# A start-order planner of a fused attention and two-layer kernel: double cost for transfers to 64 partitions, and a hold on transfers while the modelled queue is long

## The chip, the cores and the metric

One core of one Trainium2 chip. The metric is the device time of one execution in microseconds (us). The engines are called as in the profile: PE (TensorE, matmuls), PEld (its weight loads), DVE (VectorE), ACT (ScalarE), POOL (GpSimd) and SP (SyncE, which issues nearly all transfers).

## The reference

```
q, k, v: 4 x 8 x 576 x 64     s: 4 x 8 x 576
cum    = cumsum(max(s, 0))
scores = q k^T / 8 + min(cum_j - cum_i, 0), causal, then a softmax over j
x      = (attn v), heads side by side: 2304 tokens x 512
h = x w_in  (512 x 2048);  g = softplus(h);                 y   = g w_out
h = y w_in2 (512 x 2048);  g = P(h)/Q(h) (cubic/quadratic); out = g w_out2
```

All inputs are large enough in scale that the softmax is sharp. The kernel keeps matmul operands as a high part and a low part, so most products are three matmuls.

## The kernel before, in words

**Work.** 32 (batch, head) pairs of attention produce x. The first layer (`ph` 0) takes the tokens in six tiles, two of 256 and four of 448; the second (`ph` 1) takes six tiles of 384. Per tile and per block of 128 hidden columns (`ff`, 16 of them) `stage_a` (L990) makes h with 12 matmuls (L1006 to L1008), `stage1` and `stage3` the nonlinearity and its split (L1104 to L1108, L1144, L1146), `stage_b` (L1028) the second product (L1042 to L1044; L1049 to L1051 in the second layer). Attention runs alongside the first layer: the first 256 rows of batches 0 and 1 come first, since the two tiles of 256 tokens need nothing else; the other heads are spread between the blocks. A head is `scores` (L607 to L610), `softmax_rows` (DVE L587 to L602, ACT L600, POOL L603), transposes (L673 to L694) and the product with v (L732, L757).

**What arrives by transfer.** `load_pair` (L499) brings q and k of two early heads to 64 partitions (256 KB), `load_cum` (L504) two rows of running sums below them (`raw2<-cumc`, 8 KB), `load_v2` the v of eight heads (768 KB). `load_raw` (L519, transfer at L539) brings q and k of the later heads to all 128 partitions; `prep` adds rows of sums (`st<-cum_d`, L563). `load_w` (L847, transfer at L856) brings 512 KB of weights as 64-bit floats to 128 partitions; `conv_t` (L862, DVE L870 and L872, ACT L871) makes them 32-bit, and `conv_hl` splits them (ACT L881, POOL L882); low parts go out to memory at L891 and come back at L901.

**What sets the order.** The program text gives instructions and dependences. `plan` (L318) then simulates the first 600 us with costs of its own: `Step` gives each instruction a duration, `forward` (L207) starts at each step the ready instruction that can start first, by rank among equals, and `latest` (L292) makes new ranks from the latest start that each could have had. Six rounds are run and the shortest is kept. L1335 chains the instructions of every engine in that order; each engine, SP among them, runs its list in order on the chip. The planner's transfers share one line, `dma`: each starts when the line is free and takes bytes / `DMA_RATE`, and lands `DMA_LATENCY` later (L272). In `earliest` (L225) a transfer may not start before the eighth last one has landed (`LANES`). All these numbers act on the order alone.

Of the kernel before, what the change touches and what calls it, by code (L numbers as in the profile page):

```python
# [59 lines left out]
SHARED = {("two", "wide"): 0.7, ("two", "thin"): 0.25, ("one", "wide"): 0.7, ("one", "thin"): 0.3,  # L60
          ("wide", "two"): 0.2, ("wide", "one"): 0.05, ("thin", "two"): 0.6, ("thin", "one"): 0.3}
HOLD, ROUNDS = 0.0, 6
DMA_RATE, DMA_LATENCY, LANES = 320e3, 1.9, 8


class Access:


    def __init__(self, x):
        t = x.bass_ap.tensor  # L70
        dims = [tuple(d) for d in x.bass_ap.ap]
        self.tile, self.dims, off = t.name, dims, x.bass_ap.offset
        self.elements = 1
        for _, m in dims[1:]:
            self.elements *= m
        self.pool = self.psum = None
        if getattr(t, "tag_meta", None) is None or str(t.space).endswith("DRAM"):
            self.box = (0, 1, off, off + sum(s * (n - 1) for s, n in dims) + 1)
            self.ordered = "_d" in t.name
            return  # L80
        self.ordered = True
        self.pool = (str(t.tag), t.tag_meta.bufs)
        self.psum = str(t.tag).split("_")[0] in PSUM_TAGS
        row = 1
        for n in list(t.shape)[1:]:
            row *= n
        p0, f0 = divmod(off, row)
        self.box = (p0, p0 + dims[0][1], f0, f0 + sum(s * (n - 1) for s, n in dims[1:]) + 1)
        if self.psum:
            self.box = (0, 128, 0, 512)  # L90
# [10 lines left out]
class Step:  # L101


    def __init__(self, i, tied):
        self.i, self.tied = i, tied
        self.engine = str(i.engine).split(".")[-1]
        acc = [[Access(x) for x in xs if getattr(getattr(x, "bass_ap", None), "tensor", None) is not None]
               for xs in (i.outs, i.ins)]
        self.outs, self.ins = acc
        self.dma, self.port = 0, None  # L110
        n = self.outs[0].elements if self.outs else 1
        psum = any(x.psum for x in self.outs + self.ins)
        wide = len(self.ins) > 1 and self.ins[1].dims[1][1] > 1
        if "DMA" in i.opcode:
            self.dma = 4 * n * self.outs[0].dims[0][1]
            self.busy = self.done = ISSUE.get(self.engine, 0.5)
        elif self.engine == "PE":
            turn = self.ins[0].tile.startswith("ident")
            full = not turn and "32r" not in str(i.ins[0].bass_ap.dtype)
            self.busy = 0.00085 * n if turn else 0.024 + 0.00162 * n if full else 0.012 + 0.000428 * n  # L120
            self.done = self.busy + 0.165
        elif self.engine == "Activation":
            more = max(0, len(self.outs) + len(self.ins) - 2)
            near = any(x.psum for x in self.ins)
            self.busy = (0.12 + 0.00079 * n + 0.07 * more) if near else (0.165 + 0.0008 * n + 0.095 * more)
            self.done = self.busy + 0.08
        elif self.engine == "DVE" and n == 1:
            self.busy, self.done = 0.115, 0.155
        elif self.engine == "DVE":
            one = len(self.ins) < 2 and not psum and i.opcode != "TensorCopy"  # L130
            self.busy = 0.06 + 0.00064 * n if one else 0.107 + 0.00105 * n
            self.done = self.busy + 0.06
            self.port = None if psum else "one" if one else "two"
        elif self.engine == "Pool":
            self.busy = 0.22 + 0.00205 * n if wide else 0.28 + 0.0007 * n
            self.done = self.busy + 0.03
            self.port = "wide" if wide else "thin"
        else:
            self.busy = self.done = 0.1
# [39 lines left out]
class Planner:  # L179
# [27 lines left out]
    def forward(self, rank):  # L207
        steps, tiles, pool, queue = self.steps, self.tiles, self.pool, self.queue
        n = len(steps)
# [13 lines left out]
        dma, landed = 0.0, []  # L223

        def earliest(k):  # L225
            t, need = ready[k], {}
            if steps[k].dma and len(landed) >= LANES:
                t = max(t, landed[-LANES])
            for x in tiles[k]:
                if x not in held:  # L230
                    tag = pool[x][0]
                    need[tag] = need.get(tag, 0) + 1
                    ahead = queue[tag][head[tag]:head[tag] + need[tag]]
                    if any(y not in held and y not in tiles[k] for y in ahead):
                        return None
                    free = sorted(slots[tag], key=lambda q: q[0])
                    if len(free) < need[tag]:
                        return None
                    t = max(t, free[need[tag] - 1][0], last[tag])
            return t  # L240

        for _ in range(n):
            best = None
            for e in self.engines:
                can = [(max(t, clock[e]), rank[k], k) for k in wait[e] for t in (earliest(k),) if t is not None]
                if can:
                    t0 = min(can)[0]
                    pick = min((c for c in can if c[0] <= t0 + HOLD), key=lambda c: (c[1], c[0], c[2]))
                    if best is None or pick[0] < best[0]:
                        best = pick  # L250
            t, _, k = best
# [19 lines left out]
            if s.dma:  # L271
                dma = max(dma, clock[s.engine]) + s.dma / DMA_RATE  # L272
# [1123 lines left out]
```

## Time and profile before

| | |
|---|---|
| Median of 3 runs | 1045.41 us (1045.2 to 1045.7) |
| The profiled execution | 1044.85 us |
| Its span, first to last instruction | 1043.1 us |
| Instructions | 17736 |
| PE busy | 1018.0 us, 98% of the span |
| DVE, ACT, POOL busy | 784.5, 803.5, 459.4 us |
| Transfers | 138.70 MB, mean 133 GB/s |

The profiled execution is 0.56 us under the median and 1.75 us over its own span. Busy shares are averages over stages; the table of stretches tells the stages apart. A busy PE is not PE at its peak, since matmuls are pipelined and their ends are modelled. In rows of instructions the columns are start, duration, engine, line, operation, output and inputs, and in brackets the idle time of the engine before it with what ended it.

### The profile page before, as it was taken

Reading aid. Unit: us, or ns where it says so; the run is one execution under the profiler, and the core shown is the slowest. Engines: PE = TensorE matmul, PEld = TensorE weight load, DVE = VectorE, ACT = ScalarE, POOL = GpSimd, SP = SyncE. Lnnn points to the kernel's source line nnn. Section 1 sums busy time; section 2 is a strip of 40 time slices with the busy share of each in tenths; the row PEclk is TensorE's granted clock in tenths of the full one; section 3 lists DMA queues with packets and bytes.
Section 4 is the critical chain, followed back from the end, with each engine's and each line's share of the span. In section 5 each row is a group of like instructions: output and inputs, shape, how many; then the busy total and the mean of one; then the engine's idle time right before and its main releaser. Section 6 shows DMA issues by size and latency. Waiting matters only on the chain.

```text
span 1043.1 us, 17736 instructions
## 1 busy us (share of the span) xinstructions
PE 1018.0 (98%) x5764; PEld 923.3 (89%) x5764; DVE 784.5 (75%) x1858; ACT 803.5 (77%) x1693; POOL 459.4 (44%) x509
## 2 busy tenths in 40 slices
PE   6999999999999999999999999999999999999998
PEld 5889989988998888999999999989999999999996
DVE  5888877788887888885776787687676776767765
ACT  5898878887887778786566567778787887887875
POOL 2756765421221122222435775445454454444542
PEclk9999999999999999999999999999999999999999
DMA  8877566565564644435779865010010110100100
GB/s 237 298 244 240 171 211 209 176 202 155 167 180 129 207 151 139 129 107 175 246 231 324 301 181 194 1 31 31 1 62 1 31 31 1 44 18 1 31 1 31
DMA packets 67950, 138.70 MB, mean 133 GB/s; under 512 B 8336, under 2 KB 21456, under 8 KB 67856
## 3 DMA queue, kind: packets, MB, share of 16 engines
q1 hardware_dynamic: 65312, 133.39, 40.6%
q10 hardware_dynamic: 2544, 4.16, 1.5%
q8 instruction: 46, 0.75, 0.3%
q14 instruction: 48, 0.39, 0.1%
HBM read 110.82 MB, written 22.61 MB: 128 GB/s over the span
## 4 chain that ended last, share of the span: by engine, by line
PE 71%; DVE 12%; ACT 6%; DMA 4%; POOL 3%; issue 3%; SPq 0%; POOLq 0%; DVEq 0%; ACTq 0%
PE h L1007 6%; PE h L1006 6%; PE h L1008 6%; PE at L732 5%; PE acc L1049 5%; PE acc L1051 5%; PE acc L1050 5%; PE acc L1043 4%; PE acc L1042 4%; PE acc L1044 4%; PE at L1006 3%; PE at L1007 3%; PE at L1008 3%; PE at L609 3%; PE at L610 2%
## 5 line engine op out<-in xcount | busy, mean ns | idle before, releaser
L1006 PE MATMUL h<-xs,w1h 128*128 128x448 f32 (+1 forms) x352 | 120.1, 342 | 1.3 <-DVE e L1108 1.3
L1043 PE MATMUL acc<-gl,w1h 128*128 128x448 f32 (+1 forms) x352 | 119.4, 341 | 1.2 <-POOL gl L1146 1.2
L1007 PE MATMUL h<-xs,w1h 128*128 128x448 f32 (+1 forms) x352 | 119.5, 340 | 0.0
L1008 PE MATMUL h<-xs,w1l 128*128 128x448 f32 (+1 forms) x352 | 119.4, 340 | 0.0
L1042 PE MATMUL acc<-gh,w1h 128*128 128x448 f32 (+1 forms) x352 | 119.3, 341 | 0.0
L1044 PE MATMUL acc<-gh,w1l 128*128 128x448 f32 (+1 forms) x352 | 118.2, 338 | 0.1
L603 POOL TENSOR_SCALAR PA<-PA,stat 128x384 f32<-128x384 f32 (+3 forms) x112 | 71.9, 648 | 101.5 <-DVE stat L602 33.6
L1049 PE MATMUL acc<-w2h,gh 128*128 128x512 f32 x288 | 113.9, 395 | 0.1
L1051 PE MATMUL acc<-w2h,gl 128*128 128x512 f32 x288 | 113.5, 394 | 0.0
L1050 PE MATMUL acc<-w2l,gh 128*128 128x512 f32 x288 | 113.5, 394 | 0.0
L1146 POOL TENSOR_TENSOR gl<-PA,gh 128x384 fp32r<-128x384 f32 x95 | 96.7, 1018 | 6.2 <-ACT gh L1144 5.0
L1117 POOL TENSOR_TENSOR tc<-tc,e 128x384 f32<-128x384 f32 x47 | 50.8, 1082 | 98.5 <-ACT tc L1115 98.5
L603 POOL TENSOR_SCALAR P<-P,stat 128x576 f32<-128x576 f32 x32 | 26.4, 824 | 136.2 <-DVE stat L602 36.0
L600 ACT ACTIVATE PA<-PA,stat 128x384 f32<-128x384 f32 (+3 forms) x112 | 64.0, 572 | 11.5 <-DVE stat L587 9.3
L1006 PEld LDWEIGHTS h<-xs,w1h 128*128 128x128 f32 x352 | 66.3, 189 | 5.4 <-DVE e L1108 1.7
L1043 PEld LDWEIGHTS acc<-gl,w1h 128*128 128x128 f32 x352 | 66.1, 188 | 4.7 <-POOL gl L1146 1.4
L1007 PEld LDWEIGHTS h<-xs,w1h 128*128 128x128 f32 x352 | 66.2, 188 | 3.3
L1008 PEld LDWEIGHTS h<-xs,w1l 128*128 128x128 f32 x352 | 66.2, 188 | 3.3
L1044 PEld LDWEIGHTS acc<-gh,w1l 128*128 128x128 f32 x352 | 66.1, 189 | 3.4 <-POOL w1l L882 0.3
L1042 PEld LDWEIGHTS acc<-gh,w1h 128*128 128x128 f32 x352 | 66.1, 189 | 3.2
L1051 PEld LDWEIGHTS acc<-w2h,gl 128*128 128x128 f32 x288 | 54.1, 188 | 13.1 <-DVE gl L1146 0.3
L1130 DVE SCALAR_TENSOR_TENSOR tc<-tc,e 128x384 f32<-128x384 f32 x48 | 27.5, 574 | 50.4 <-ACT e L1129 48.6
(235 smaller groups left out, 3209.0 us busy)
## 6 DMA issues: line engine op xcount, KB each, us to landing
w1l<-l_d SPq DMA_DIRECT2D x138, 256.0 KB
raw<-in_w_dram SPq DMA_DIRECT2D x48, 512.0 KB
raw<-in_qk_dram SPq DMA_DIRECT2D x24, 384.0 KB
l_d<-w1l SPq DMA_DIRECT2D x32, 256.0 KB
raw64x<-in_w_dram SPq DMA_DIRECT2D x16, 512.0 KB
raw<-in_qk_dram SPq DMA_DIRECT2D x8, 576.0 KB
w_d<-PA SPq DMA_DIRECT2D x16, 256.0 KB
R<-in_vv_dram SPq DMA_DIRECT2D x12, 320.0 KB
```

Of the source, the lines that this page charges most:

```text
L600: nc.scalar.activation(pt[:, 0:n], pt[:, 0:n], AF.Exp, bias=mn, scale=-1.0, accum_out=stat[:, i, 1:2])
L603: nc.gpsimd.tensor_scalar(pt[:, 0:n], pt[:, 0:n], stat[:, i, 2:3], 1.0, op0=ALU.mult, op1=ALU.mult)
L1006: nc.tensor.matmul(h, wh[:, cs], xh, start=(k == 0), stop=False)
L1007: nc.tensor.matmul(h, wh[:, cs], xl, start=False, stop=False)
L1008: nc.tensor.matmul(h, wl[:, cs], xh, start=False, stop=(k == KD - 1))
L1042: nc.tensor.matmul(o, wh[:, cs], gh, start=first and not both, stop=False)
L1043: nc.tensor.matmul(o, wh[:, cs], gl, start=False, stop=False)
L1044: nc.tensor.matmul(o, wl[:, cs], gh, start=False, stop=last and (not both or m % 2 == 1))
L1049: nc.tensor.matmul(acc[m], gh[:, cs], wh, start=first, stop=False)
L1050: nc.tensor.matmul(acc[m], gh[:, cs], wl, start=False, stop=False)
L1051: nc.tensor.matmul(acc[m], gl[:, cs], wh, start=False, stop=last)
L1146: eng.tensor_tensor(gl, g, f(gh), op=ALU.subtract)
```

## The change

Three edits in the planner, none in the kernel's own instructions. The rate of its transfer line goes from 320e3 to 400e3 bytes per us. A transfer whose output has 64 to 127 rows counts double bytes: the pair loads and the few transfers that write half a tile. And a transfer may not start until the line's end is at most 1.5 us ahead (`BACKLOG`), so that in the simulation a transfer that becomes ready meanwhile can go first.

```diff
-DMA_RATE, DMA_LATENCY, LANES = 320e3, 1.9, 8
+DMA_RATE, DMA_LATENCY, LANES, BACKLOG = 400e3, 1.9, 8, 1.5
...
         if "DMA" in i.opcode:
-            self.dma = 4 * n * self.outs[0].dims[0][1]
+            rows = self.outs[0].dims[0][1]
+            self.dma = 4 * n * rows * (2 if rows in range(64, 128) else 1)
...
         def earliest(k):
             t, need = ready[k], {}
-            if steps[k].dma and len(landed) >= LANES:
-                t = max(t, landed[-LANES])
+            if steps[k].dma:
+                t = max(t, dma - BACKLOG)
+                if len(landed) >= LANES:
+                    t = max(t, landed[-LANES])
```

No instruction is added or removed; the five engines' lists are permuted. Of some 5600 instructions of PE the moves end at about the 3000th, and few are over 35 places; SP's list is the same in most of its second half. Three places follow. Lines of the changed file below the edits are 3 higher than before.

SP near the start of the program, before, and then with the change. `raw64_...` are weights, `raw2_...` early pairs (64 rows) and their rows of sums (2 rows, from `cumc`), `prm` the six coefficients of the second layer:

```order
L856 DMA raw64_1874<-in_w1_dram 128x1024
L856 DMA raw64_2030<-in_w1_dram 128x1024
L1326 DMA prm_125<-in_ab_dram 128x6
L505 DMA raw2_133<-cumc_149 2x1024
L505 DMA raw2_135<-cumc_149 2x1024
L505 DMA raw2_137<-cumc_149 2x1024
L501 DMA raw2_331<-in_qk0_dram 64x1024
L505 DMA raw2_331<-cumc_149 2x1024
L856 DMA raw64_165<-in_w1_dram 128x1024
L856 DMA raw64_167<-in_w1_dram 128x1024
L501 DMA raw2_429<-in_qk0_dram 64x1024
```

```order
L859 DMA raw64_1874<-in_w1_dram 128x1024
L508 DMA raw2_133<-cumc_149 2x1024
L508 DMA raw2_135<-cumc_149 2x1024
L508 DMA raw2_137<-cumc_149 2x1024
L504 DMA raw2_331<-in_qk0_dram 64x1024
L508 DMA raw2_331<-cumc_149 2x1024
L504 DMA raw2_429<-in_qk0_dram 64x1024
L859 DMA raw64_165<-in_w1_dram 128x1024
L859 DMA raw64_167<-in_w1_dram 128x1024
L508 DMA raw2_429<-cumc_149 2x1024
```

The second 512 KB of weights and `prm` have left the place ahead of the rows of sums (they now stand 16 places later, after the first large head), and the pair load `raw2_429` has passed the weights `raw64_165` and `raw64_167`, which are the first to be converted.

DVE where the first h tile `h_511` gets its softplus (L1108, then L1111); L587 (then L590) is the row reduction of a head, L870 (then L873) and L872 (then L875) convert weights. Before, and then with the change:

```order
L587 ISA PA_563,stat_562<-acc_564,mask_123 128x256
L587 ISA stat_562 128x1
L870 TENSOR_SCALAR tc_436<-raw64_371 128x512
L870 TENSOR_SCALAR tc_470<-raw64_397 128x512
L587 ISA PA_605,stat_604<-acc_606,mask_123 128x128
L587 ISA stat_604 128x1
L601 TENSOR_SCALAR stat_562<-stat_562 128x1
L587 ISA PA_605,stat_604<-acc_606,mask_123 128x256
L587 ISA stat_604 128x1
L1108 SCALAR_TENSOR_TENSOR e_551<-h_511,e_551 128x256
```

```order
L590 ISA PA_563,stat_562<-acc_564,mask_123 128x256
L590 ISA stat_562 128x1
L1111 SCALAR_TENSOR_TENSOR e_551<-h_511,e_551 128x256
L875 SCALAR_TENSOR_TENSOR tc_436<-raw64_371,tc_436 128x512
L604 TENSOR_SCALAR stat_562<-stat_562 128x1
L590 ISA PA_605,stat_604<-acc_606,mask_123 128x128
```

The softplus of the first tile now stands ahead of the reductions of `PA_605` and of one conversion (`tc_470`).

SP in the stretch where the last weights of the first layer and the heads of batch 1 come in (`raw_2021`, `raw_2116`, `raw_2182` are q and k of heads). Before, and then with the change:

```order
L539 DMA raw_2021<-in_qk_dram 128x704
L856 DMA raw64_2344<-in_w1_dram 128x1024
L856 DMA raw64_2355<-in_w1_dram 128x1024
L563 DMA st_2074<-cum_d_63 4x704
L891 DMA l_d11_1_87<-w1l_2357 128x512
L891 DMA l_d14_0_92<-w1l_2498 128x512
L539 DMA raw_2116<-in_qk_dram 128x704
L563 DMA st_2148<-cum_d_63 4x704
L545 DMA R_2487<-in_vv_dram 128x640
L545 DMA vr_2023<-in_vv_dram 128x384
L539 DMA raw_2182<-in_qk_dram 128x704
L856 DMA raw64_2495<-in_w1_dram 128x1024
```

```order
L859 DMA raw64_2355<-in_w1_dram 128x1024
L542 DMA raw_2021<-in_qk_dram 128x704
L548 DMA R_2487<-in_vv_dram 128x640
L894 DMA l_d14_0_92<-w1l_2498 128x512
L894 DMA l_d12_1_89<-w1l_2508 128x512
L859 DMA raw64_2495<-in_w1_dram 128x1024
L566 DMA st_2074<-cum_d_63 4x704
L894 DMA l_d15_0_94<-w1l_2661 128x512
L542 DMA raw_2116<-in_qk_dram 128x704
L566 DMA st_2148<-cum_d_63 4x704
```

Weights and the stores of low parts have moved ahead of the heads' q and k: `raw64_2495` is 4 places earlier in SP's list, `raw_2116` 4 places later; six heads in this stretch go 3 or 4 places back in the same way.

## Rows read from the trace of the kernel before

**Rows 1.** The page: busy tenths and the granted clock in 40 slices.

```profile
PE   6999999999999999999999999999999999999998
PEclk9999999999999999999999999999999999999999
DMA  8877566565564644435779865010010110100100
```

**Rows 2.** Stretches of 25 us: busy us (instructions), granted clock, DMA share, GB/s.

```profile
core 0: us, PE busy (x) PEld busy (x) DVE busy (x) ACT busy (x) POOL busy (x), PEclk, DMA share, GB/s
0.00:25.00 25.00, 16.23 (x59) 12.84 (x59) 13.59 (x67) 12.54 (x37) 7.59 (x25) 1.00 0.89 240
25.00:50.00 25.00, 22.93 (x153) 20.02 (x153) 21.00 (x88) 22.25 (x68) 17.98 (x25) 1.00 0.88 289
...
175.00:200.00 25.00, 23.23 (x184) 22.33 (x183) 17.96 (x56) 20.08 (x51) 10.60 (x12) 1.00 0.50 153
200.00:225.00 25.00, 25.00 (x166) 22.59 (x164) 21.43 (x62) 22.16 (x48) 7.57 (x9) 1.00 0.83 246
...
575.00:600.00 25.00, 25.00 (x125) 23.08 (x124) 20.25 (x23) 13.18 (x24) 20.11 (x18) 1.00 0.90 307
```

**Rows 3.** PE's waits of the whole run: us in total, times, longest us.

```profile
PE acc L607 <- DMA raw<-in_qk_dram: 5.1, 1, 5.1
PE at L689 <- POOL PA L603: 3.0, 5, 0.8
PE at L694 <- POOL P L603: 2.5, 4, 1.1
PE acc L673 <- POOL gh L603: 2.2, 1, 2.2
PE at L607 <- DMA raw<-cumc: 1.4, 1, 1.4
PE h L1006 <- DVE e L1108: 1.3, 2, 0.9
PE acc L1043 <- POOL gl L1146: 1.2, 1, 1.2
```

**Rows 4.** Chain that ended last, from 7 to 16 us: start, us, what.

```profile
7.25 0.81 ACT cumc L455
...
8.09 6.25 DMA raw<-cumc
14.34 0.04 issue
14.38 1.65 PE at L607 x4
```

**Rows 5.** SP's instructions in order of time, 4 to 13 us.

```profile
4.24 0.58 SPq L512 DMA_DIRECT2D v<-in_v_dram  x1
4.87 0.91 SPq L856 DMA_DIRECT2D raw<-in_w_dram  x2
5.82 0.43 SPq L1326 DMA_DIRECT2D prm<-in_ab_dram  x1
8.09 1.98 SPq L505 DMA_DIRECT2D raw<-cumc  x3
```

**Rows 6.** Stretches of 2 us near the start; the last figure is GB/s.

```profile
4.00:6.00 2.00, 0.85 (x3) 0.89 (x4) 1.01 (x4) 0.81 (x1) 0.00 (x0) 1.00 0.93 214
6.00:8.00 2.00, 2.00 (x6) 1.15 (x5) 1.96 (x5) 0.75 (x1) 0.00 (x0) 1.00 1.17 231
10.00:12.00 2.00, 1.76 (x7) 1.34 (x8) 0.26 (x2) 0.67 (x2) 2.00 (x8) 1.00 1.02 409
12.00:14.00 2.00, 0.94 (x2) 0.22 (x2) 0.00 (x0) 0.31 (x1) 0.30 (x1) 1.00 1.06 292
```

**Rows 7.** DVE and PE in the chain, 38 to 42 us.

```profile
38.64 1.55 DVE tc L870 x2
...
40.46 0.33 DVE PA L587
...
40.80 0.35 DVE e L1108
...
41.19 0.39 PE h L1006
```

**Rows 8.** DVE, 159 to 166 us.

```profile
159.23 0.85 DVE L872 SCALAR_TENSOR_TENSOR tc<-raw,tc 128x512 int32<-128x512 int32 x1
...
165.46 0.43 DVE L870 TENSOR_SCALAR tc<-raw 128x512 int32<-128x512 int32 x1 [1.63 <-DMA raw<-in_w_dram]
```

**Rows 9.** SP, 153 to 161 us, and ACT's conversion of the head loaded at 153.48.

```profile
153.48 0.33 SPq L539 DMA_DIRECT2D raw<-in_qk_dram  x1
...
159.14 0.33 SPq L539 DMA_DIRECT2D raw<-in_qk_dram  x1
160.10 0.33 SPq L856 DMA_DIRECT2D raw<-in_w_dram  x1
...
161.13 0.79 ACT L564 ACTIVATE ht<-raw 128x704 fp32r<-128x704 f32 x1
```

**Rows 10.** DVE's first conversion of weights, in order of time.

```profile
20.10 0.42 DVE L870 TENSOR_SCALAR tc<-raw 128x512 int32<-128x512 int32 x1
```

**Rows 11.** The chain's transfer for a head at 153 us.

```profile
153.48 2.64 DMA raw<-in_qk_dram
```

## The prediction

> **What bounds the kernel now.** I read the page first. PE is busy in nine tenths or more of every slice after the first, at the full granted clock throughout, and the transfers fill up to nine tenths of their time early and hardly anything in the last two fifths [rows 1]. The stretches of 25 us divide the run. From 200 us on PE is busy in all 25.00 of 25 us, also where transfers are at 0.90 of their time, so there the kernel is bound by PE, and the change removes no PE instruction. Before that it is not full: 16.23 us in the first stretch, 22.93 in the second, 23.23 in the eighth [rows 2]. So all that an order can win lies in the first 200 us, and what is won there reaches the end, since the work behind it is PE work of fixed length. PE's waits give the size of the prize: 5.1 us for the first transfer and sums, 3.0 and 2.5 us for POOL's scaling of softmax rows ahead of transposes, 2.2 for the first such scaling, 1.4 for a transfer of running sums, 1.3 for the softplus on DVE, 1.2 for a split on POOL [rows 3]. That is 16.7 us, and only the 1.4 names a transfer that the change moves. The change gives a better price to transfers and a better order to SP; it can't make the waits for POOL and ACT work shorter except by chance.
>
> **Term 1, the start.** The running sums are ready at 7.25 + 0.81 = 8.06 us, the transfer that carries them is issued at 8.09, and it lands after 6.25 us, at 14.34; PE starts the third head at 14.38 [rows 4]. The transfer is 8 KB. It is late because of what SP issued ahead of it: pairs, v, two weight loads of 512 KB between 4.87 and 5.78, and the coefficients [rows 5]. The change takes the second weight load and the coefficients out from in front, so the rows of sums land sooner by the time of 512 KB. Between 10 and 12 us, where full-width weights are moved, the queue carries 409 GB/s, which makes 524288 / 409000 = 1.28 us; between 12 and 14 us, with the end of that load in it, it carries 292, which makes 1.80 us [rows 6]. The wanted load straddles both; I take 1.5 us. PE's wait of 1.4 us [rows 3] isn't the limit: between 12 and 14 us PE has 0.94 us of other work [rows 6], and in its new list the third head's scores stand ahead of the last of it. Bounds: 0 if DVE and POOL, busy 21.00 and 17.98 of the next 25 us [rows 2], lose the lead again; 1.8 if all is kept.
>
> The weights left out are for a block late in the first layer. That they come 16 places later costs nothing while the loads between keep the queue full, as they do: the DMA share in the first two stretches is 0.89 and 0.88 [rows 2]. The cover is the DMA queue's own backlog; were it gone, the price would be one load, 1.28 us, on SP's next weights. Behind it on SP stand four weight loads whose order and bytes ahead are the same as before. The coefficients are first read on DVE and ACT, and both readers move far back with them.
>
> **Term 2, the first softplus.** PE waits for e at L1108 before it can reuse a bank of h: twice in the run, the longest 0.9 us [rows 3]. In the chain, L1108 at 40.80 stands right behind a reduction of a head (0.33) and shortly behind two conversions of together 1.55 us, and PE's L1006 follows at 41.19 [rows 7]. The change puts the reductions of one head (at least 0.33) and one of the two conversions (half of 1.55, 0.78) behind L1108: 1.1 us sooner on DVE, against 0.9 us of waiting. Part of it will be used up by ACT, whose list also changes there. I take 0.5 us, bounds 0 and 0.9. What is moved behind is late next: a conversion for the second half of a block, and the reductions of one head.
>
> **Term 3, the last weights.** At 165.46 DVE has waited 1.63 us for weights [rows 8] that SP issued at 160.10 [rows 9], just after the 0.85 us conversion that frees their buffer, 159.23 to 160.08 [rows 8]. This load is 4 places earlier in SP's list, but a place alone gives nothing while the buffer is held; conversions too move up, by 2 to 4 places on POOL. Bounds 0 and 1.63; I take 0.4, nearer to 0 because of the buffer.
>
> **Sum.** 1.5 + 0.5 + 0.4 = 2.4 us less. Made on the profiled execution, 1044.85 - 2.4 = 1042.45; that execution is 0.56 us under the median, so the median would be 1045.41 - 2.4, about **1043.0 us**. With the bounds of the three terms alone, 0 to 4.3 us less.
>
> **A rule on partitions.** At 4 to 8 us, while pairs to 64 partitions are moved, the queue carries 214 and 231 GB/s with its engines counted as 0.93 to 1.17 busy, about half of the 409 at 10 to 12 us [rows 6]; so doubling these bytes is right for them. [...]
>
> **Rival A, the lead is not passed on.** The first converted weights, `raw64_165`, lose 512 KB in front and get a pair of 256 KB in its place, 262144 / 222500 = 1.18 us at the mean of the two rates [rows 6] against 1.28. They arrive only 0.1 us sooner. If they gate the first layer, the heads run ahead for nothing and 0.1 us is left: 1045.3 us. With half of term 1 kept it would be 1044.6. For it: DVE is busy 21.00 of 25 us behind the start [rows 2], and the change moves the first h tile behind heads on PE. Against it: DVE's first conversion at 20.10 shows no wait for its weights [rows 10]. Chance 0.28.
>
> **Rival B, slower: heads late behind weights.** Six heads' q and k move 3 or 4 places back in SP's list, behind weights, stores that wait for POOL, and rows of sums. The load at 153.48 takes 2.64 us [rows 11] and ACT uses it at 161.13 [rows 9]: a slack of 161.13 - 153.48 - 2.64 = 5.0 us. Four places later in the old list is 159.14 [rows 9], a slip of 5.66 us. This decides from a slip of 5.0 us: each head then waits 0.65 us, and as the next load needs the buffer that this one frees, the waits add up, 6 x 0.65 = 3.9 us. With term 1 kept, 1045.41 - 1.5 + 3.9 = 1047.8 us. For it: these loads already stand in the chain that ended last [rows 11], and PE was not full there [rows 2]. Against it: weights ahead free SP of its own waits, and the slip can be shorter than in the old list. Chance 0.18.
>
> **Rival C, the order is better all along.** If the truer prices also halve PE's waits for POOL's scaling, (3.0 + 2.5) / 2 = 2.7 us [rows 3], the sum is 5.1 us: 1040.3 us. For it: the list is permuted up to about the 3000th PE instruction. Against: those waits come from POOL, ACT and DVE, whose costs aren't changed. Chance 0.14.
>
> **Rival D, it does nothing that counts.** The hold is only in the simulation; on the chip SP issues the next transfer as soon as its own wait is over, and no queue is kept short. If the moves cancel out, 1045.4 us. Chance 0.07.
>
> **How the numbers follow.** The forecast has 0.33. About 0.2% (2.1 us) is what a measurement of this kernel can tell from no change. Forecast and C are faster by more: 0.47. A and D lie within it: 0.35. B is slower by more: 0.18. The range runs from 1039.0, C with another 1.3 us (0.4 more in term 2 and 0.9 more in term 3, within their bounds), to 1047.3, B with its waits a little under the full 0.65 us each; about one in eight lies above it, and a small rest below. The forecast alone would have 1041.1 to 1045.4, the bounds of its terms.
>
> **What would show it.** Term 1 is right if PE starts the third head at 12.6 to 13.1 us instead of 14.38, and if the transfer of sums takes about 4.7 us instead of 6.25 in the chain. Term 2 is right if the first L1111 ends before 40 us and PE's wait for it is under 0.9 us. Term 3 is right if DVE's wait for weights near 165 us is gone. Rival A would show as a new wait of DVE L873 for weights near 20 us, or as PE busy less than 22.93 us between 25 and 50. Rival B would show as waits of ACT L567 for `raw<-in_qk_dram` between 110 and 200 us and a lower PE share there. The forecast is wrong if PE's first full stretch begins no earlier than before, or if its waits for L603 grow by more than 2 us.

## The result and the profile after

The changed kernel is slower: 1056.26 us median (1054.14 to 1058.95, 4 runs) against 1045.31 (1044.16 to 1045.70, 4 runs) of before on the same chip, ratio 1.0108 [1.0093, 1.0124]. Forecast were 1043.0 us and a range up to 1047.3. The profiled execution took 1054.14 us, with a span of 1052.3; it is the fastest of the four, 2.1 us under their median. Lines of the code stand 3 further down than before; in some of the experiments they shift by more, and there the names of the tiles tell what a row is.

The stretches of the changed kernel (columns as in [rows 2]):

```profile
0.00:25.00 25.00, 15.66 (x54) 12.36 (x55) 12.50 (x59) 10.91 (x32) 7.67 (x23) 1.00 0.87 233
25.00:50.00 25.00, 20.93 (x130) 18.27 (x129) 20.62 (x82) 20.03 (x59) 19.43 (x24) 0.93 0.74 251
...
175.00:200.00 25.00, 24.00 (x198) 23.71 (x197) 17.96 (x59) 20.44 (x51) 8.62 (x11) 1.00 0.50 154
200.00:225.00 25.00, 24.89 (x166) 22.74 (x166) 20.95 (x61) 21.15 (x47) 9.47 (x9) 1.00 0.74 230
575.00:600.00 25.00, 23.30 (x112) 20.47 (x111) 15.53 (x19) 12.01 (x23) 15.68 (x14) 1.00 0.92 317
```

Two places differ most from [rows 2]. In the second stretch PE executes 130 matmuls instead of 153, and its granted clock is 0.93, no longer 1.00. At 575 to 600 us, where PE had been full, it executes 112 instead of 125. PE's waits of the whole run (columns as in [rows 3]):

```profile
PE acc L610 <- DMA raw<-in_qk_dram: 5.1, 1, 5.1
PE at L697 <- POOL P L606: 3.6, 5, 1.5
PE acc L610 <- DVE stat L590: 2.2, 1, 2.2
PE acc L760 <- ACT pt L658: 2.2, 4, 0.6
PE h L1009 <- DVE e L1111: 2.1, 3, 0.9
...
PE at L610 <- DMA raw<-cumc: 1.6, 1, 1.6
```

New are 2.2 us for a reduction and 2.2 for ACT's copies `pt`. The wait for e (the softplus step) is 2.1 instead of 1.3 [rows 3], but 1.7 of it stand at the late place, around 590 us, and 0.4 at 638.78 us; near 40 us PE no longer waits for e at all. Now the chain that ended last (start, us, what):

```profile
7.94 5.00 DMA raw<-cumc
12.94 0.04 issue
12.98 1.65 PE at L610 x4
14.63 1.28 PE acc L760 x4
15.91 2.56 PE acc L610 x8
18.47 0.23 PE h L676
18.70 0.02 issue
18.72 0.50 ACT pt L658
...
36.98 1.46 POOL w1l L885
38.44 2.18 POOL PA L606 x2
40.63 0.74 POOL cum L494
...
43.12 0.28 DVE PA L590
```

The transfer of sums takes 5.00 us instead of 6.25, and the third head starts at 12.98 instead of 14.38 [rows 4]. The lead is spent at 18.5 us, where eight score matmuls stand ahead of the second head's last transpose, and ACT's copy and PE's next product come behind it. At 37 to 43 us the chain goes through POOL, first the weights, then a head, then the sums (`cum`), and only then through the reductions (`PA L590`) that PE needs. PE at that place:

```profile
43.80 1.23 PE L610 MATMUL acc<-raw 66*128 66x128 f32 x4 [2.24 <-DVE stat L590]
```

and the clock around it, in stretches of 5 us:

```profile
40.00:45.00 5.00, 2.76 (x16) 2.24 (x15) 4.02 (x10) 3.25 (x10) 4.33 (x4) 0.93 0.82 263
45.00:50.00 5.00, 5.00 (x31) 4.72 (x30) 3.03 (x18) 3.76 (x11) 3.95 (x6) 0.73 0.94 300
```

At the late place, PE and then POOL:

```profile
590.06 0.47 PE L1009 MATMUL h<-xs,w1h 128*128 128x448 f32 x1 [0.78 <-DVE e L1111]
596.12 0.47 PE L1009 MATMUL h<-xs,w1h 128*128 128x448 f32 x1 [0.88 <-DVE e L1111]
```

```profile
582.41 0.65 POOL L877 TENSOR_SCALAR raw<-raw 128x512 f32<-128x512 f32 x1 [3.46 <-DMA raw<-in_w_dram]
584.15 1.01 POOL L877 TENSOR_SCALAR raw64x<-raw64x 128x512 f32<-128x512 f32 x1 [1.10 <-DMA raw64x<-in_w_dram]
```

```profile
588.00 0.43 DVE L878 TENSOR_SCALAR tc<-raw64x 128x512 int32<-128x512 int32 x1 [2.30 <-POOL PA L885]
589.40 0.61 DVE L1111 SCALAR_TENSOR_TENSOR e<-h,e 128x448 f32<-128x448 f32 x1
```

POOL stands still for second-layer weights that have not landed; the conversions L878 to L880 on DVE wait for POOL, the softplus step L1111 is listed behind them, and PE needs its result to reuse a bank. POOL's waits for these weights between 573 and 606 us, before and then changed:

```profile
POOL raw64x L874 <- DMA raw64x<-in_w_dram: 0.7, 1, 0.7
POOL raw L874 <- DMA raw<-in_w_dram: 0.7, 1, 0.7
```

```profile
POOL raw L877 <- DMA raw<-in_w_dram: 4.2, 3, 3.5
POOL raw64x L877 <- DMA raw64x<-in_w_dram: 2.2, 2, 1.1
```

A measure for the experiments is the **lag**: by how much the n-th matmul of a run starts later than the n-th of before, both counted from the first, which is number 0. As the orders differ, and with them which matmuls come first, a lag at 55 us need not be a loss: latency_2.0 is 4.1 behind there and 0.9 ahead at 448, where the orders have nearly joined again. One profiled execution each; the ratio comes from all runs:

| run | ratio to before | 240th (55 us) | 2800th (448) | 3400th (563) | 3600th (604) | last |
|---|---|---|---|---|---|---|
| changed | 1.0108 [1.0093, 1.0124] | 5.5 | 5.0 | 6.1 | 8.7 | 9.3 |
| new_to_60 | 1.0049 [1.0035, 1.0062] | 6.4 | 5.7 | 5.7 | 5.7 | 5.5 |
| old_to_60 | 1.0044 [1.0029, 1.0059] | 1.3 | 2.5 | 3.2 | 6.8 | 7.0 |
| new_to_450 | 1.0081 [1.0053, 1.0108] | 7.6 | 10.2 | 11.5 | 11.5 | 11.8 |
| old_to_450 | 1.0034 [1.002, 1.0047] | -0.4 | -1.2 | -0.9 | 3.8 | 3.9 |
| rate_only | 1.0076 [1.0052, 1.01] | 5.0 | 5.8 | 6.9 | 10.7 | 10.6 |
| double_alone | 1.0041 [1.0026, 1.0056] | 6.4 | 5.0 | 5.1 | 5.1 | 5.4 |
| hold_alone | 1.0038 [1.0025, 1.0051] | 4.6 | 3.2 | 3.2 | 3.2 | 5.6 |
| sums_back | 1.01 [1.008, 1.012] | 4.4 | 5.1 | 6.2 | 11.8 | 11.3 |
| weights_only | 1.0045 [1.0028, 1.0061] | 3.3 | 5.0 | 4.9 | 5.3 | 5.3 |
| heads_only | 1.007 [1.0053, 1.0087] | 5.4 | 7.7 | 8.0 | 8.7 | 9.5 |
| sums_only | 1.0065 [1.0047, 1.0083] | 6.9 | 6.1 | 6.1 | 6.5 | 7.2 |
| lead_only | 0.9998 [0.9987, 1.0009] | 0.0 | -0.2 | -0.2 | 1.1 | 1.6 |
| rate_300 | 0.999 [0.9978, 1.0003] | 1.1 | -2.5 | -2.1 | -1.9 | -2.0 |
| rate_310 | 0.9986 [0.9977, 0.9996] | -0.1 | -3.3 | -3.0 | -2.7 | -2.7 |
| rate_330 | 1.0006 [0.9991, 1.0021] | 0.5 | -0.3 | 0.6 | 0.8 | 2.1 |
| rate_350 | 1.0094 [1.0075, 1.0113] | 3.7 | 5.6 | 6.2 | 8.4 | 9.9 |
| latency_1.8 | 1.008 [1.005, 1.011] | 3.2 | 5.0 | 4.9 | 4.9 | 7.0 |
| latency_2.0 | 0.9988 [0.9979, 0.9997] | 4.1 | -0.9 | -0.6 | -0.3 | -1.3 |

For the changed kernel the table says: 5.5 us are lost by 55 us, nothing between there and 448, 1.1 near 481 (one wait for POOL's scaling of a head), and 2.6 from 563 to 604.

Executions of one order differ as well. new_to_450, one of the experiments below, lists on every engine the same instructions in the same order as the changed kernel up to 480 us, yet its profiled execution, the slowest of its four (3.4 us over their median), is 2.1 us further behind at 55 us and 5.2 at 448. What a part of the change costs is therefore read from the ratios, and the lag tells where, if several executions agree. At the start they do: the three with the changed start (changed, new_to_60, new_to_450) are 5.5 to 7.6 us behind at 55 us, the two others with the start of before (old_to_60, old_to_450) -0.4 to 1.3.

### The profile page after: what moved, and what is told of

Same layout as the page of the kernel before. It is cut to its first block, busy times and chain, and to the rows that moved or that the text cites. A ratio compares the mean times of both kernels' runs of the same rounds, so it can differ in the third digit from the quotient of the medians.

```text
span 1052.3 us, 17742 instructions
## 1 busy us (share of the span) xinstructions
PE 1022.6 (97%) x5764; PEld 926.0 (88%) x5764; DVE 788.4 (75%) x1858; ACT 802.3 (76%) x1693; POOL 461.4 (44%) x509
## 4 chain that ended last, share of the span: by engine, by line
PE 68%; DVE 12%; ACT 7%; DMA 5%; POOL 4%; issue 3%; SPq 0%; POOLq 0%; DVEq 0%; ACTq 0%
PE h L1009 6%; PE h L1010 6%; PE h L1011 6%; PE at L735 5%; PE acc L1052 5%; PE acc L1054 5%; PE acc L1053 5%; PE acc L1045 4%; PE acc L1046 4%; PE acc L1047 4%; PE at L1010 3%; PE at L1009 3%; PE at L1011 3%; PE at L612 2%; PE at L613 2%
## 5 line engine op out<-in xcount | busy, mean ns | idle before, releaser
L1009 PE MATMUL h<-xs,w1h 128*128 128x448 f32 (+1 forms) x352 | 121.1, 344 | 1.7 <-DVE e L1111 1.7
L1009 PEld LDWEIGHTS h<-xs,w1h 128*128 128x128 f32 x352 | 66.8, 190 | 6.2 <-DVE e L1111 3.0
L1054 PEld LDWEIGHTS acc<-w2h,gl 128*128 128x128 f32 x288 | 54.1, 188 | 13.1 <-DVE gl L1149 0.3
L1053 PEld LDWEIGHTS acc<-w2l,gh 128*128 128x128 f32 x288 | 54.2, 188 | 12.5
```

The costliest lines, as they stand in the source:

```text
L1009: nc.tensor.matmul(h, wh[:, cs], xh, start=(k == 0), stop=False)
L1053: nc.tensor.matmul(acc[m], gh[:, cs], wl, start=False, stop=False)
L1054: nc.tensor.matmul(acc[m], gl[:, cs], wh, start=False, stop=last)
```

## Experiments

The expectations name these theories. S: the start is lost where the long sums chain stands between the heads. L: the late place is lost because second-layer weights are listed too early. M: the loss is spread over many small places. After the first runs: W, the first layer's weights are listed too late; H, the heads' own order; R, any order other than before's loses; and last O, an order planned with transfers that land too soon loses.

### Where the loss lies: start and late place apart

Four kernels join the order of one planner setting up to a time of the plan with the order of the other behind it. OLD is before's setting, NEW the changed one. The first, new_to_60:

```diff
+    p, first, start = lines_by(NEW, instructions, tied)
+    _, then, start2 = lines_by(OLD, instructions, tied)
...
+        head = [k for k in first[e] if start[k] < 60.0]
+        tail = [k for k in then[e] if k not in done and start2[k] < until]
```

> Orders spliced at 60 us of the planner's time: what the changed planner puts there in the first 60 us, and behind it the order of before, so PE differs from before up to its 235th place alone. The trace of the change lags the one of before by 5.3 us at its 240th to 320th matmul and by 9.3 us at the end. Theory S (start): the first 60 us hold the larger part of the loss, through running sums (L491 to L495) moved into the reductions of heads: 5 to 6 us slower than before, ratio 1.005. Theory L (late): what counts are second-layer weights taken up too early near 580 us: 0 to 1 us, ratio 1.000. Theory M (middle): losses arise anew everywhere from many small moves: under 3 us here.

Measured: 1.0049, 6.4 us lost by 55 us, nothing behind, as theory S said. The mirror, old_to_60:

```diff
+    p, first, start = lines_by(OLD, instructions, tied)
+    _, then, start2 = lines_by(NEW, instructions, tied)
```

> The mirror image: the order of before in the first 60 us of the planner's time, the changed planner's order behind it. Theory S with a late part: 4 to 5 us slower than before, the lag arising at 481 and at 575 to 600 us (1.1 and 3.2 us in the trace of the change), ratio 1.004. Theory L: nearly all of the loss, 8 to 11 us, ratio 1.009. Theory M: 6 us or more, spread over 60 to 450 us.

Measured: 1.0044, with 3.6 us between 563 and 604. The two losses, 0.49 and 0.44%, add up to 0.93% of the 1.08, each good to about 0.15. So there are at least two causes, not one that starts the other. Third, new_to_450:

```diff
-        head = [k for k in first[e] if start[k] < 60.0]
+        head = [k for k in first[e] if start[k] < 450.0]
```

> The changed planner's order in the first 450 us of the planner's time, the order of before behind it. Theory S with a late part: the lag of the start stays, 5 us, and the steps at 481 and 575 to 600 us are gone, ratio 1.005. Theory L: 0 to 2 us. Theory M: as slow as the first splice plus what the middle adds, 6 us or more.

Measured: 1.0081; the step at 563 to 604 is gone (11.5 and 11.5), the one near 481 is not. Theory S had 1.005; the loss of 8.2 us is inside theory M's 6 us or more. Its trace loses 2.6 us between 55 and 448 us, where the trace of the changed kernel, with the same order, loses none. So a third, smaller loss may lie between 60 and 450 us of the plan (1.0081 against 1.0049, with intervals that overlap); it isn't resolved. Fourth, its mirror old_to_450 (OLD first, then NEW):

```diff
+        head = [k for k in first[e] if start[k] < 450.0]
```

> Order of before up to 450 us of the planner's time, the changed planner's order behind it. The mirror of new_to_450. Theory L (second-layer weights are taken too early at 575 to 603 us, because the planner counts 400 GB/s where the trace shows 290 to 320): PE loses 3 to 4 us there, no other stretch loses, no half clock before the end; ratio 1.003 to 1.0045. Theory M (the loss is spread over many small places): ratio under 1.002, since most of its places are cut off. Rival R (any other order than that of before loses, wherever it differs): also over 1.003, but with the loss not in 575 to 603 us.

Measured: 1.0034, inside what theory L gave for the late place alone. Up to the 3400th matmul it runs as before; then PE waits four times, in order of time:

```profile
578.23 0.47 PE L1024 MATMUL h<-xs,w1h 128*128 128x448 f32 x1 [1.20 <-DVE e L1126]
584.30 0.47 PE L1024 MATMUL h<-xs,w1h 128*128 128x448 f32 x1 [0.93 <-DVE e L1126]
590.37 0.47 PE L1024 MATMUL h<-xs,w1h 128*128 128x448 f32 x1 [0.92 <-DVE e L1126]
600.89 0.47 PE L1024 MATMUL h<-xs,w1h 128*128 128x448 f32 x1 [0.48 <-DVE e L1126]
```

and its POOL waits there for weights in the same way:

```profile
POOL raw L892 <- DMA raw<-in_w_dram: 6.9, 4, 4.1
POOL raw64x L892 <- DMA raw64x<-in_w_dram: 1.5, 1, 1.5
```

### The late place: the raised rate

```diff
-DMA_RATE, DMA_LATENCY, LANES = 320e3, 1.9, 8
+DMA_RATE, DMA_LATENCY, LANES, BACKLOG = 400e3, 1.9, 8, float("inf")
-            self.dma = 4 * n * rows * (2 if rows in range(64, 128) else 1)
+            self.dma = 4 * n * rows * (1 if rows in range(64, 128) else 1)
```

> Only the rate of the planner's transfer line is raised, 320e3 to 400e3; no doubling, no hold. Theory: the late loss comes from the rate, since the queue moves 290 to 320 GB/s near 580 us and the planner now expects weights sooner than they come: 3 to 4 us slower than before near 580 us, ratio 1.003 to 1.004, and the start as before. Rival: the hold, which lets other transfers pass, makes the late loss, and the rate alone does nothing or is faster, ratio 0.998 to 1.001.

Measured: 1.0076, with 3.8 us at the late place, as the theory said; but the start, which it expected as before, is 5.0 us behind at 55 us. All kernels whose late order was planned at 400 GB/s lose 2.6 to 5.6 us between the 3400th and the 3600th matmul (changed, old_to_60, old_to_450, sums_back, rate_only); these five have the same list there on PE, DVE and POOL. rate_350 loses 2.2; the thirteen others, planned there at 300 to 330, lose 0 to 1.3, doubling and hold alone among them. The late loss is therefore the rate's, and this cause is shown: the transfers move 307 GB/s there in the trace of before [rows 2] and 317 in the changed one, and a plan at 400 lists conversions ahead of data that come at under four fifths of that.

### The start: sums, weights or heads?

The changed kernel lists the long sums chain between the reductions of two heads, where PE stands still for 2.24 us. sums_back puts it at before's places and nothing else (the keys that order each engine's list):

```diff
+    key = [other[k] if sums(x) else start[k] for k, x in enumerate(p.steps)]
```

> The changed kernel with one thing put back: the ten or so instructions of make_cum (DVE scan and multiply-add, POOL subtract and scale, ACT copy and row writes, the store of cum_d) stand where the planner of before put them, ahead of the reductions of heads 5 and 6; all other instructions keep the changed kernel's order on every engine. Theory S (the start is lost because this chain moved in between the heads' reductions, which leaves TensorE idle for 2.4 us near 42 us and brings the half clock after it): PE's gap near 42 us is under 1 us, the first stretch of half clock (44 us) is gone, and of the changed kernel's +10.9 us some 2.5 to 5 come back, ratio to before 1.006 to 1.0085. If S is wrong (the head reorder itself loses the start, sums or not): ratio stays 1.0093 to 1.0124 and a gap of 2 us is still in 38 to 46 us.

Measured: 1.01, the loss stays. The gap at 42 us is gone, but PE waits earlier instead:

```profile
32.85 0.92 PE L817 MATMUL at<-pt,v 128*128 128x256 f32 x4 [2.03 <-ACT pt L715]
```

So the first theory of the start fell: putting the sums back doesn't give the loss back, it only moves PE's wait. The three thirds of new_to_60, each moved alone into before's order, use the same line, with `sums(x)` true for the weight path of the first layer (weights_only), for the heads (heads_only) or for the sums (sums_only). For the first two it is bounded to the first 60 us; sums_only keeps the line above:

```diff
-    key = [other[k] if sums(x) else start[k] for k, x in enumerate(p.steps)]
+    key = [other[k] if sums(x) and min(other[k], start[k]) < 60.0 else start[k] for k, x in enumerate(p.steps)]
```

> The order of before, with only the first layer's weight path of the first 60 us of the planner's time put where the changed planner puts it: the loads of w1 and of the a, b table, their conversions on DVE, ACT and POOL, the spilled halves, and the first-layer matmuls and softplus steps. Heads and sums keep before's places. With heads_only and sums_only it divides the order of new_to_60 (ratio 1.0049) in three. Theory W (the changed planner believes that w1 lands some 4 us later, because the heads' 64-partition loads ahead of it count double and new loads are held; it so lists the first conversions to w1h and the first-layer matmuls 4 us later than the data allow, and PE has nothing to fill the heads' waits with): first-layer matmuls start at 33 to 36 us instead of 30.6, PE is 3 to 5 us behind before by the 240th matmul, ratio 1.003 to 1.0055. If W is wrong: lag within 1.5 us, ratio 0.999 to 1.0015.

> The order of before, with only the heads' steps of the first 60 us (pair loads, rows of sums into the pairs, scores, reductions, softmax, transposes, products with V) where the changed planner puts them; weights, first layer and the long sums chain keep before's places. Theory H (the heads' own new order, transposes behind eight more score matmuls, loses the start): PE 3 to 5 us behind by the 240th matmul, ratio 1.003 to 1.0055. Theory W: the heads' lead of Term 1 is kept, lag between -1.5 and +1 us, ratio 0.998 to 1.001; this would then be the part of the change worth keeping.

> The order of before, with only the long sums chain (make_cum) at the changed planner's places, between the reductions of heads 5 and 6. Theory S in its first form: PE idle over 2 us near 42 us and half clock behind it, ratio 1.002 to 1.005. Theories W and H: lag under 1 us, ratio 0.999 to 1.0015. The run that put the sums back in the changed kernel kept the loss (1.01), so S alone is not expected to hold; this run tells whether the chain's place costs anything where weights and heads stand well.

Measured: 1.0045, 1.007 and 1.0065. Each third alone loses about as much as all three together or more (1.0049), in a wait of its own. sums_only moves no matmul at all: PE's list is the one of before, and a few dozen places on DVE and ACT, and fewer on POOL and SP, cost 0.65%. Of weights_only, heads_only and sums_only:

```profile
29.45 0.33 PE L734 MATMUL acc<-ident,gh 128*128 128x128 f32 x1 [1.44 <-POOL gh L664]
```

```profile
33.69 0.92 PE L818 MATMUL at<-pt,v 128*128 128x256 f32 x4 [1.96 <-ACT pt L716]
```

```profile
32.99 0.73 PE L1086 MATMUL acc<-w1h,pth 128*128 128x512 f32 x2 [2.90 <-ACT w1h L941]
```

Theories W, H and S each expected one third to carry the loss and the others to be free. None holds. W's own run came out in its range, but not by its mechanism: the first layer's matmuls start at 31.66 us, not at 33 to 36. A third taken out of its plan may collide with the rest of the other plan, so these runs can't tell which third is to blame. The two other parts of the change, alone. double_alone:

```diff
-            self.dma = 4 * n * self.outs[0].dims[0][1]
+            self.dma = 4 * n * rows * (2 if rows in range(64, 128) else 1)
```

> The old rate (320e3), no hold; only the doubling for transfers to 64 to 127 partitions is kept. The order differs from before's in more rows than the changed kernel's does (DVE 1808 rows of difference, POOL 423), but the scan of make_cum stands at its old place (66 on DVE, before 65, changed 88) and the second-layer weights on POOL are within two places of before's. Theories S and L together: no half clock near 44 us, no loss at 575 to 603 us; ratio 0.998 to 1.003. Rival R (any re-dealt order loses): 1.004 to 1.010.

hold_alone:

```diff
+                t = max(t, dma - BACKLOG)
```

> The old rate, no doubling, only the hold of 1.5 us. By theory W the hold alone keeps back little, since without doubling the planner's queue is hardly ever 1.5 us long ahead of the first weights: ratio 0.999 to 1.003. Rival R: 1.003 to 1.009, as for any other order. Theory L: no loss at 575 to 604 us.

Measured: 1.0041 and 1.0038. Both are over what theories S, L and W gave (up to 1.003) and inside the range of rival R. double_alone is 5.0 us behind at 448 us and 5.4 at the end; hold_alone is 3.2 us behind at 448 us and loses another 2.4 behind 604, where PE waits 1.39 us for e at 634.81. Neither loses at the late place. In double_alone PE stands still where POOL converts weights and the sums ahead of a head's scaling:

```profile
34.65 0.90 PE L676 MATMUL h<-ident,gh 128*128 128x128 f32 x3 [2.45 <-POOL gh L606]
```

### Term 1 alone

lead_only keeps before's order in everything but one row of SP: the second early weight load goes 17 places back.

```diff
+    key = [other[k] if sums(x) and start[k] < 10.0 and other[k] > 15.0 else start[k] for k, x in enumerate(p.steps)]
```

> The order of before on every engine, but for one row of SP: the second of the two weight loads of 512 KB that stand ahead of the rows of sums (for a late block of the first layer, tile raw_2030) goes 17 places back, behind the last pair, as in the changed order. Term 1 alone. If Term 1 is passed on: third head at 12.9 to 13.1 us instead of 14.38, PE 1 to 1.5 us ahead at the 240th matmul and at the end, ratio 0.9985 to 0.999. Rival A (not passed on): third head early, but lag back to 0 by 45 us, ratio 0.9995 to 1.0005. Rival R's strongest form (any touch of this start loses): ratio over 1.002.

Measured: 0.9998 [0.9987, 1.0009]. The full 1.5 us (0.9986) lies just outside the interval, the range given for rival A (not passed on) holds the value, and the trace decides for rival A. PE is 1.2 us ahead at the 80th matmul (29.5 us) and 0.0 at the 160th. Between them:

```profile
13.40 1.65 PE L668 MATMUL at<-raw 66*128 66x128 f32 x4 [0.49 <-DMA raw<-cumc]
...
33.10 0.39 PE L1068 MATMUL h<-xs,w1h 128*128 128x256 f32 x1 [1.13 <-DVE xs L824]
```

The head comes 0.98 us sooner than in [rows 4], and 20 us later PE waits 1.13 us for DVE's split of a head's output, a wait that the trace of before doesn't show there.

### Does any other order lose as much?

Six kernels change one number of before's planner that adds no knowledge of the chip, without doubling and hold. rate_330, then latency_1.8, latency_2.0 and rate_310, last rate_300 and rate_350:

```diff
-DMA_RATE, DMA_LATENCY, LANES = 320e3, 1.9, 8
+DMA_RATE, DMA_LATENCY, LANES = 330e3, 1.9, 8
```

> Before's planner with its transfer rate at 330e3 in place of 320e3, nothing else: a 3 per cent change of one cost that says nothing new of the chip, yet re-deals many rows (PE 2648 rows of difference, DVE 1307, SP 408). Sums at the old place (65), second-layer weights as before but for two places. Theories S and L: ratio 0.999 to 1.0025. Rival R (before's order is a favourable draw, and any change of a cost that re-deals the rows loses about as much): 1.004 to 1.008, with half clock somewhere in the first 130 us.

```diff
+DMA_RATE, DMA_LATENCY, LANES = 320e3, 1.8, 8
```

> Before's planner with its fixed transfer latency at 1.8 us in place of 1.9, nothing else. A second change of a cost that says nothing new of the chip, but re-deals about as many rows as the change under study (PE 3247 rows of difference, DVE 1578). Theories W and L: ratio 0.998 to 1.003, since all transfers shift alike and no step is listed 4 us off. Rival R (any order that is dealt anew this widely loses about as much as the change): 1.004 to 1.010.

```diff
+DMA_RATE, DMA_LATENCY, LANES = 320e3, 2.0, 8
```

> Before's planner with its fixed transfer latency at 2.0 us in place of 1.9, nothing else (PE 1773 rows of difference, DVE 897). A third change of a cost that says nothing of the chip. Rival R: ratio 1.003 to 1.009, the lag made before 160 us. Theories W, H and S: 0.998 to 1.003.

```diff
+DMA_RATE, DMA_LATENCY, LANES = 310e3, 1.9, 8
```

> Before's planner with a rate of 310e3 in place of 320e3, nothing else (PE 1768 rows of difference, DVE 710). A fourth such change. Rival R: ratio 1.003 to 1.009, the lag made before 160 us. Theories W, H and S: 0.998 to 1.003. No loss at 575 to 604 us by either (theory L has the raised rate as its cause).

```diff
+DMA_RATE, DMA_LATENCY, LANES = 300e3, 1.9, 8
```

> Before's planner with a rate of 300e3, nothing else (PE 3636 rows of difference, DVE 1100). Theory O: not slower than before, 0.996 to 1.001; second-layer weights are listed later still, nothing lost at 575 to 604 us. Rival R: as likely as not over 1.003, with the lag made before 160 us.

```diff
+DMA_RATE, DMA_LATENCY, LANES = 350e3, 1.9, 8
```

> Before's planner with a rate of 350e3, nothing else (PE 3687 rows of difference, DVE 1436). Theory O: slower, 1.002 to 1.007, lag made before 160 us. Theory L by its dose: the second-layer weights on POOL stand between before's places and the changed ones (284, 287, 288, 293 where before has 286, 287, 289, 293 and the change 284, 285, 288, 291), so PE loses 0 to 2 us at 575 to 604 us. Rival R: as likely as not within 0.2% of before or faster, as with 330e3.

Measured, with PE's one wait for the rows of sums near 13 us, of which before has 1.4 [rows 3]:

| setting | ratio | wait for `raw<-cumc`, us |
|---|---|---|
| 300e3 | 0.999 | 0.8 |
| 310e3 | 0.9986 | 0.8 |
| latency 2.0 | 0.9988 | 1.2 |
| before, 320e3 and 1.9 | 1 | 1.4 |
| 330e3 | 1.0006 | 1.2 |
| latency 1.8 | 1.008 | 2.6 |
| 350e3 | 1.0094 | 3.7 |
| 400e3 (rate_only) | 1.0076 | 6.4 |

The row of the waits of rate_310, of rate_350 and of rate_only:

```profile
PE at L610 <- DMA raw<-cumc: 0.8, 1, 0.8
```

```profile
PE at L610 <- DMA raw<-cumc: 3.7, 1, 3.7
```

```profile
PE at L610 <- DMA raw<-cumc: 6.4, 1, 6.4
```

Rival R in its plain form (any other order loses) falls with latency_2.0, rate_310, rate_300 and rate_330, which re-deal rows by the thousand and are not slower; latency_1.8 came out as R said. Theory O, a plan that takes data for landed too soon loses, was formed from the first of these runs. Of the two later ones rate_300 came out in its range (0.999 in 0.996 to 1.001), rate_350 on its side but with more than it gave (1.0094 against 1.002 to 1.007). All three settings with later landings are level or 0.1% faster; of the four with earlier ones three lose 0.8 to 0.9% and one nothing. A weaker form of R stays: before's order is a good draw, and more than half of all others lose. Were the three losers among these seven dealt by chance, all three would fall on the four earlier settings in 4 of 35 cases. The loss doesn't grow evenly with the rate (350e3 loses about as much as 400e3), which also speaks for a good part of luck in its size.

The wait for the sums goes with the loss, but it doesn't measure it and doesn't show the mechanism. In rate_only PE waits 5.0 us longer than in before, yet the third head starts at 14.19 us, sooner than in before (14.38 [rows 4]):

```profile
14.19 0.80 PE L610 MATMUL at<-raw 66*128 66x128 f32 x2 [6.45 <-DMA raw<-cumc]
```

PE stands still there because its list has the head next and other work behind it, and it makes up for much of this: at the 80th matmul (29.5 us) rate_only is 2.1 us behind and rate_350 2.0, but so is latency_2.0 (2.0), which ends 1.3 us ahead.

rate_310 has the lowest ratio of the study: 1043.03 us median of 10 runs, 0.9986 [0.9977, 0.9996], 0.14% faster than before, with PE busy 24.11 of 25 us in the second stretch against 22.93 [rows 2]. latency_2.0 and rate_300 can't be told from it.

**What stays open.** Why the start loses isn't shown. Theory O doesn't explain it alone: the changed kernel's wait for the sums is 1.6 us against 1.4 before, and doubling and hold, which make transfers later in the plan, still lose 0.4% each. That they shift some transfers against others, and so list the first weights' conversions too late, was argued and not shown: weights_only, the run that was to show it, lost 0.45%, but so did the two thirds that it was to be told from.

## Why the prediction was wrong

**Term 1 (-1.5 us)** was right in what it said and wrong in what it is worth. The transfer took 5.00 us (said: about 4.7), the third head started at 12.98 (said: 12.6 to 13.1). Alone, with the one weight load moved, it is worth 0.2 us with an interval of about ±1.1 (lead_only). The failed step is the one that took PE's wait of 1.4 us as a loss that ends with it. It was slack for the next late thing, DVE's work for `xs`. Its lower bound, 0 if DVE and POOL lose the lead again, was the value.

**Rival A** named this outcome for term 1, with the wrong gate: not the first converted weights, but DVE's `xs` in lead_only, and in the changed kernel ACT's copy at 18.72. Its sign, PE busy less than 22.93 us between 25 and 50, came (20.93), but with a kernel 10.9 us slower, where A had it level. Of the two signs by which the forecast was to fall one came (PE, full from 200 us on in before, is full from 225 on) and the other, longer waits for POOL's scaling, did not.

**Term 2 (-0.5 us)** failed. The softplus step was to end before 40 us; it ran at 43.67 in the changed trace, behind the sums and the reductions of a head. PE's wait for it near 40 us is gone, as the term said, but only because PE now waits 2.24 us for those reductions just ahead. The step that failed counted the rows that move behind it on DVE, and not those ahead of it that came later: the sums' multiply-add on DVE waited for POOL, and POOL had weights and a head in front of it.

**Term 3 (-0.4 us):** DVE's wait for weights at 165.46 us [rows 8] is gone, and at 164.74 it waits 1.15 us for ACT in its place:

```profile
164.74 1.03 DVE L875 SCALAR_TENSOR_TENSOR tc<-raw,tc 128x512 int32<-128x512 int32 x1 [1.15 <-ACT raw L874]
```

**Rival B** was the only slower case, at 1047.8 us. Its sign, ACT's waits for `raw<-in_qk_dram` between 110 and 200 us, isn't in the trace of the changed kernel, and the lag there is 5.5 at 55 us and 5.0 at 448. **Rivals C and D** did not come.

**Two steps failed, and they make most of the error.** First, "all that an order can win lies in the first 200 us" holds for winning, not for losing: PE full at 575 to 600 us [rows 2] meant that the conversions behind it were covered, and the change took that cover away. This place was put at nothing and costs 0.34 to 0.44% (old_to_450, old_to_60). The rows for it stood in the prediction's own list, 307 GB/s where those weights come [rows 2] and 409 only between 10 and 12 us [rows 6]; the raised rate was treated as a truer price, though those rows show it for two microseconds. Second, the cost of a start that is dealt anew was set to the few moves that were followed. That start costs 0.49% (new_to_60), about 5 us. With every engine working in its listed order, moves that were not followed made a wait of 2.24 us for DVE and four of together 2.2 for ACT, and a stretch at a granted clock of 0.50, 45 to 47 us, behind the first; which of the moves is to blame stays open. Rival C gave such moves a gain of 2.7 us. Of the ten planner settings that were timed beside before's, six lost 0.38% or more and the best gained 0.14%. (Two readings of its first paragraph are also a little off: the last slice of [rows 1] has 8 tenths, and behind 625 us PE of before is busy in 412.23 of 418 us, not in all. Nothing hung on them.)

**The rule on partitions** rests on [rows 6] alone, the rates while pairs move, 214 and 231 GB/s, and while full-width weights do, 409. It told nothing of the time: the kernel with the doubling alone is 0.41% slower. A truer price of one kind of transfer was no better order here.

## What to carry to other kernels

In a kernel whose engines work off a list planned beforehand, take the transfer rate from the stretch in which the plan's data come, and round it down rather than up: here plans at 300 to 330 GB/s, near the 307 of the crowded stretch, were level or 0.1% faster, and 350 and 400 lost 0.8 to 0.9%. At the late place this is shown; for the start it is a pattern of seven settings of one kernel. Look for losses where the bound engine is full as well: here the cover of its feeders went there, at 0.34 to 0.44%. Before a term is counted for an earlier arrival, move that one row by itself: a lead of 1.2 us was worth nothing 20 us later. Before a lag of a few microseconds is explained, take a second profile of the same order: two differed here by 5 us.

## What the runs showed of the hardware

TensorE's granted clock fell behind some of the new waits, and in the changed kernel this made a wait dearer than its length. There PE waited 2.24 us until 43.80; then the granted clock was 0.50 of full over 45 to 47 us and 0.73 over 45 to 50, and L1009, the same product with 256 columns, took 0.21 us in the chain where at 34.99 it took 0.12:

```profile
34.99 0.12 PE h L1009
...
45.04 0.21 PE h L1009
```

A lower clock also followed waits of 2.90 us (sums_only, 0.79 over 35 to 40 us) and 1.50 us (old_to_60, 0.71 over 110 to 115 us), but not waits of 1.44 and 1.50 us in weights_only, whose granted clock was 1.00 over the whole run, or the wait of 2.03 in sums_back, with 1.00 over 30 to 50 us; nor does before show it behind its waits of 5.1 and 2.2 us in the first 25 us [rows 2, 3]. A loss of this size at the start came without the lower clock too: weights_only and hold_alone are 5.0 and 3.2 us behind at 448 us with 1.00 over the whole run, and rate_300, whose granted clock averaged 0.995 over its profiled execution against 0.996 in the changed kernel, isn't slower than before (0.999).

And a profiled run can differ from another of the same order, by 5.2 us at 448 us in the pair named under the table. lead_only has before's order behind 60 us, yet its lag grows by 1.3 us between 563 and 604. A step of that size in one profile alone is no evidence; the late loss is read from six kernels against thirteen, and from the ratio of old_to_450.
